# The filter's response of a long convolution as eight quarter products per pair instead of four products with a block matrix

## The chip, the cores and the metric

The kernel runs on one core of a Trainium2 chip. The metric is the device time of one execution in microseconds; smaller is better. TensorE has two rows in the profile: PE, the matmuls, and PEld, the loads of their stationary operands. An fp32 matmul leaves two PE records and two PEld records.

## The reference

Only the first part matters here; a five-tap gate and two 128x128 projections follow it.

```
h_filt = (maximum(pos_emb @ w1, 0) @ w2) * exp(-0.01 * pos)     # [S, D]
u = x * v                                                       # [B, S, D]
y = irfft(rfft(u, 2S) * rfft(h_filt, 2S))[:, :S]                # causal convolution along S
attn = x * y
out = (sigmoid(conv5(attn)) * (attn @ w_val)) @ w_out
B, S, D = 4, 12800, 128;  filter_order = 64
```

## The kernel before

S is split as J x N1 x N2 = 2 x 100 x 64. The kernel has three stages, each with PSUM and SBUF pools of its own, and in each the order of instructions is the order of the code (a manual schedule).

Stage 1 transforms u along N1 and writes the spectra to a_u in HBM. Beside it, it makes ag, the filter's spectrum before the product with w2: for each of the 100 values of k1 a block whose 128 partitions are (j, e), with j the half of S and e one of the 64 hidden units, and whose 128 columns are real and imaginary part (c) of 64 frequencies.

Stage 2 is where the change lies. It loops over 50 pairs of k1. For pair p it does the following, and work of three neighbouring pairs is in flight at once:

- `filter_pair` (L358) makes the filter's response h = w2^T ag for both k1 of the pair. The weights matrix w2bd is 128 x (2 x 128): w2 stands in rows 0 to 63 for j = 0 and in rows 64 to 127 for j = 1, the other half is zeros. Four matmuls of 128 rows, 64 columns of stationary data and 256 streamed columns write one PSUM bank of the pool z_ps. ScalarE (ACT) copies it to h_sb in three instructions (L368, L369 with a sign, L370).
- `spectrum` (L373) finishes the transform of u: two matmuls into one bank of z_ps, four times per pair: z00 (called by `first`), z01 (by `second`), z10 and z11. Each matmul has 128 rows and 64 columns; the two of a spectrum lie beside each other in the array.
- `times` (L379) multiplies spectra and response on VectorE (DVE): va and vb of 2048 elements per partition from z00 and z01, vc and vd of 1024 from z10 and z11. All read one operand from PSUM.
- GpSimd (POOL) adds: L463 the first half of va and vb, L464 vc and vd, L465 the second half of va and vb. DVE then adds the second half of va to vc (L454), from SBUF into SBUF.
- `inverse` (L399) transforms back: from the first half of va (j = 0) and from vc (j = 1), four matmuls of 64 rows and 128 columns each into a two-bank tile of the pool c_ps, and ACT copies the tile to c_sb (L411), which goes to HBM by DMAs on ACT's queue (L414).

The loop's body for p runs on TensorE as z10, z11 of p; the inverse of va of p-1; the response of p+1; z00 of p+1; the inverse of vc of p-1; z01 of p+1. On DVE the row is va, vb of p; L454 of p-1; vc, vd of p. On POOL it is L463, L464, L465 of p. L454 of p-1 needs L465 of p-1.

Stage 3 reads c_y and makes gate and projections. It isn't touched.

Of PSUM z_ps holds four banks (bufs=4, five allocations per pair before the change: h and four spectra) and c_ps two tiles of two banks (bufs=2, two allocations per pair).

Of the kernel before, what the change touches and what calls it, by code (L numbers as in the profile page):

```python
# [9 lines left out]
F32 = mybir.dt.float32  # L10
F32R = mybir.dt.float32r
I32 = mybir.dt.int32
AF = mybir.ActivationFunctionType
# [10 lines left out]
B, S, D, FO, KC = 4, 12800, 128, 64, 5  # L24
J, N1, N2 = 2, 100, 64
# [91 lines left out]
def tile_longconv_gate(  # L117
# [20 lines left out]
    nc = tc.nc  # L138
# [18 lines left out]
    w2bd = const.tile([128, J, D], F32, name="w2bd")  # L157
# [22 lines left out]
    ag = ag_pool.__enter__().tile([128, N1, J, FO], F32, name="ag")  # L180
# [168 lines left out]
    with tc.tile_pool(name="p2", bufs=1) as p2, tc.tile_pool(name="ps2", bufs=1, space=PSUM) as ps2:  # L349
        BD = B * D  # L350
        NP = N1 // 2
        PG = KG // 2
        half = [slice(h * N2, (h + 1) * N2) for h in range(2)]

        def bank():
            return ps2.tile([128, BD], F32, name="z_ps", bufs=4)

        def filter_pair(p):  # L358

            h_ps = bank().rearrange("p (c e) -> p c e", c=2)  # L360
            for c in range(2):
                for h in range(2):
                    nc.tensor.matmul(
                        out=h_ps[half[h], c], lhsT=ag[:, 2 * p + h].rearrange("p j e -> p (j e)")[:, half[c]],
                        rhs=w2bd.rearrange("p j d -> p (j d)"), start=True, stop=True)
            h_sb = p2.tile([128, 2, J, 2, D], F32, name="h_sb2", bufs=3)
            src = h_ps.rearrange("p c (j d) -> p c j d", j=J)
            nc.scalar.copy(out=h_sb[:, 0].rearrange("p j c d -> p c j d"), in_=src)  # L368
            nc.scalar.activation(h_sb[:, 1, :, 0], src[:, 1], AF.Copy, scale=-1.0)  # L369
            nc.scalar.copy(out=h_sb[:, 1, :, 1], in_=src[:, 0])  # L370
            return h_sb

        def spectrum(a2, wk, j, c):  # L373
# [48 lines left out]
        def start_pair(p):  # L422
            filt_p[p] = filter_pair(p).rearrange("p s j c d -> p s (j c) d")
# [9 lines left out]
        with tc.manual_schedule():  # L433
            for p in range(-1, NP + 1):
# [4 lines left out]
                if now:  # L439
                    h = filt_p.pop(p)  # L440
# [35 lines left out]
    with tc.tile_pool(name="p3", bufs=1) as p3, tc.tile_pool(name="ps3", bufs=1, space=PSUM) as ps3:  # L476
# [140 lines left out]
        with tc.manual_schedule():  # L617
# [4 lines left out]
            for _ in range(WARM):  # L622
                w_ps = ps3.tile([D, 2 * D], F32, name="o_ps", bufs=2)
                nc.tensor.matmul(
                    out=w_ps, lhsT=ident, rhs=dft.rearrange("p a k -> p (a k)"), start=True, stop=True)
            for t in range(-AHEAD3, NT + 2):
# [3 lines left out]
                if 0 <= s < NT:  # L630
                    j, g = y_order[s]
# [75 lines left out]
```

## Time and profile before

| what | value |
|---|---|
| median of 3 runs | 1259.43 us (1249.71, 1259.43, 1262.13) |
| the profiled execution | 1253.43 us, of it the span 1251.4 us |
| mean granted TensorE clock | 0.942 |
| stage 2, about | 389 to 832 us of the span |
| busy share of the span | PE 86%, DVE 81%, POOL 70%, ACT 45% |

A profile line of a time table gives start, duration, engine, line, operation, output<-inputs, partitions x elements and count, and in brackets the idle time of the engine before it with what ended it. Matmul ends are modelled by the profile, so starts are compared here.

### The profile page before, as it was taken

The page shows a single profiled execution, that of the slowest core. Times are in us where ns is not written, and L with a number is a line of the kernel's source. Part 1 is how long each engine was busy: PE and PEld are TensorE (multiplying, and loading weights), DVE is VectorE, ACT ScalarE, POOL GpSimd, SP SyncE. Part 2 cuts the span into 40 slices and gives each one's busy share as a digit, 9 for nine tenths or more (in the row PEclk, how much of TensorE's full clock was granted, in tenths as well). Part 3 has the DMA queues.
Part 4 walks back from the last instruction along what each step waited for, and adds up shares of the span by engine and source line. Part 5 has one row for each costly group of instructions (what it writes and reads, how often), then busy time and mean ns, then how long its engine had stood idle before and what let it go on. Part 6 is the DMA issues. An engine that isn't in the chain of part 4 may idle for free. (4 is left out here: it accounts for less than half of the span.)

```text
span 1251.4 us, 15855 instructions
## 1 busy us (share of the span) xinstructions
PE 1073.3 (86%) x5244; PEld 470.7 (38%) x5244; DVE 1014.8 (81%) x1074; ACT 558.7 (45%) x936; POOL 874.0 (70%) x410
## 2 busy tenths in 40 slices
PE   1777787755676999999999999978999999999986
PEld 0544454322333333333333333343444444444432
DVE  7665444747795999999999999933999999999997
ACT  0114433523442333333343333314667667667663
POOL 2435444423452899999999999944888988988980
PEclk9889888858878999999999999988999999999999
DMA  7999999978877687788777777549999999999942
GB/s 181 270 293 360 315 314 304 307 220 275 300 258 280 226 301 274 278 289 285 280 275 272 269 279 273 202 174 258 250 283 278 294 266 269 293 277 281 294 142 106
DMA packets 86794, 333.03 MB, mean 266 GB/s; under 512 B 10062, under 2 KB 11258, under 8 KB 72378
## 3 DMA queue, kind: packets, MB, share of 16 engines
q1 hardware_dynamic: 52736, 252.34, 65.0%
q10 hardware_dynamic: 33978, 79.67, 17.3%
q8 instruction: 44, 0.72, 0.2%
q14 instruction: 36, 0.29, 0.1%
HBM read 200.90 MB, written 131.07 MB: 265 GB/s over the span
## 5 line engine op out<-in xcount | busy, mean ns | idle before, releaser
L565 POOL TENSOR_TENSOR ext<-yr,xr 128x400 f32<-128x400 f32 x120 | 299.4, 2497 | 48.0 <-DVE yr L563 44.8
L286 POOL TENSOR_TENSOR f<-u 128x512 f32<-128x512 f32 x128 | 166.1, 1320 | 219.1 <-DVE u L278 198.5
L296 PE MATMUL fp<-f,fold 64*128 64x512 f32 x512 | 160.3, 738 | 101.9 <-POOL f L286 47.6
L580 DVE SCALAR_TENSOR_TENSOR gt<-ext,cw,gt 128x1600 f32<-128x1600 f32 x128 | 242.6, 1895 | 1.6 <-ACT gt L577 1.6
L411 ACT COPY c_sb<-c_ps 128x1024 f32<-128x1024 f32 x100 | 101.3, 1013 | 270.5 <-PE c_ps L404 266.9
L376 PE MATMUL z_ps<-ld 128*64 128x512 f32 x800 | 194.9, 607 | 6.7 <-DMA ld<-a_u 6.6
L463 POOL TENSOR_TENSOR va<-va,vb 128x1024 f32<-128x1024 f32 x50 | 159.5, 3190 | 38.8 <-DVE vb L381 19.5
L299 ACT COPY st<-fp 128x1024 f32<-128x1024 f32 x64 | 64.8, 1012 | 211.5 <-PE fp L296 110.2
L538 PE MATMUL sd<-ld,inv 100*64 100x512 f32 x512 | 130.1, 612 | 9.4 <-DMA ld<-c_y 8.7
L381 DVE TENSOR_TENSOR vb<-z_ps,h_sb 128x2048 f32<-128x2048 f32 x50 | 114.6, 2291 | 25.2 <-ACT c_sb L411 24.9
L599 PE MATMUL o_ps<-gd,wout 128*128 128x400 f32 x256 | 112.3, 520 | 17.9 <-DVE gd L594 10.4
L464 POOL TENSOR_TENSOR vc<-vc,vd 128x1024 f32<-128x1024 f32 x50 | 118.1, 2361 | 8.7 <-DVE vd L381 3.4
L381 DVE TENSOR_TENSOR va<-z_ps,h_sb 128x2048 f32<-128x2048 f32 x50 | 114.1, 2282 | 11.6 <-PE z_ps L376 11.1
L278 DVE TENSOR_TENSOR u<-ld 128x1024 f32<-128x1024 f32 x64 | 80.6, 1261 | 47.3 <-DMA ld<-in_xv_dram 44.7
L465 POOL TENSOR_TENSOR va<-va,vb 128x1024 f32<-128x1024 f32 x50 | 118.6, 2371 | 0.0
L545 ACT COPY sd_sb<-sd 128x512 f32<-128x512 f32 x128 | 76.2, 595 | 88.1 <-PE sd L538 71.2
L296 PEld LDWEIGHTS fp<-f,fold 64*128 64x128 f32 x512 | 53.2, 217 | 159.2 <-POOL f L286 81.9
L589 PE MATMUL v_ps<-ext,wval 128*128 128x400 f32 x256 | 107.9, 504 | 0.0
L404 PE MATMUL c_ps<-vc,ld 64*128 64x512 f32 x400 | 101.6, 627 | 7.0 <-DVE vc L454 7.0
L301 DVE COPY st<-fp 128x1024 f32<-128x1024 f32 x64 | 78.1, 1220 | 31.7 <-DMA a_u<-st 20.4
L404 PE MATMUL c_ps<-va,ld 64*128 64x512 f32 x400 | 99.4, 615 | 0.1
L376 PEld LDWEIGHTS z_ps<-ld 128*64 128x64 f32 x800 | 54.8, 138 | 111.8 <-issue 86.6
(73 smaller groups left out, 1531.7 us busy)
## 6 DMA issues: line engine op xcount, KB each, us to landing
c_y<-c_sb ACTq DMA_DIRECT2D x100, 512.0 KB
ld<-a_u SPq DMA_DIRECT2D x49, 1024.0 KB
ld<-in_xv_dram SPq DMA_DIRECT2D x64, 768.0 KB
a_u<-st SPq DMA_DIRECT2D x64, 768.0 KB
ld<-c_y SPq DMA_DIRECT2D x128, 384.0 KB
xr<-in_xt_dram SPq DMA_DIRECT2D x32, 800.0 KB
out_dram<-o_sb ACTq DMA_DIRECT2D x32, 800.0 KB
ld<-in_tab_w_dram SPq DMA_DIRECT2D x12, 1024.0 KB
```

The costliest lines, as they stand in the source:

```text
L286: nc.gpsimd.tensor_tensor(f[:, c], u[:, :, 0], u[:, :, 1], op=op)
L296: nc.tensor.matmul(out=fp[:, h], lhsT=fold[r, c], rhs=f[r, c], start=True, stop=True)
L376: nc.tensor.matmul(out=z[half[h]], lhsT=wk[:, h, half[c]], rhs=a2[:, h, j], start=True, stop=True)
L381: nc.vector.tensor_tensor(out, z.rearrange("p (b d) -> p b d", d=D).unsqueeze(1).to_broadcast([128, n, B, D]), h_sb.unsqueeze(2).to_broadc ...
L404: nc.tensor.matmul(out=c_ps[:, h], lhsT=wk[half[h], 2 + c], rhs=vt[half[h], c].rearrange("p b d -> p (b d)"), start=(c == 0), stop=(c == 1))
L463: nc.gpsimd.tensor_tensor(va[:, 0:2], va[:, 0:2], vb[:, 0:2], op=ALU.add)
L464: nc.gpsimd.tensor_tensor(vc, vc, vd, op=ALU.add)
L465: nc.gpsimd.tensor_tensor(va[:, 2:4], va[:, 2:4], vb[:, 2:4], op=ALU.add)
L538: nc.tensor.matmul(out=sd[c * N2:(c + 1) * N2], lhsT=inv[:, c], rhs=ct[c][:, r * B * D:(r + 1) * B * D], start=True, stop=True)
L565: nc.gpsimd.tensor_tensor(e[:, r0 + r], yr, xr, op=ALU.mult)
L580: nc.vector.scalar_tensor_tensor(gt, rows(t, k), cw[:, k:k + 1], gt, op0=ALU.mult, op1=ALU.add)
L599: nc.tensor.matmul(out=o_ps, lhsT=wout, rhs=gd, start=True, stop=True)
```

## The change

The response is made by eight matmuls: each takes 64 rows (one j) and 64 columns (one of c), streams only the 128 columns of w2 that aren't zero, and writes half the partitions of one bank. The two j go to the two banks of a tile from the pool c_ps; the columns 256 to 511 of each bank stay unused. The pool z_ps is left with four allocations per pair, and c_ps has three. ACT's three copies read the new tile in its own order; their element counts stay 512, 256 and 256 per partition. The lines after the new code are one higher: L363 becomes L364, L368 to L370 become L369 to L371, L404 becomes L405, L454 becomes L455 and so on.

```
-            h_ps = bank().rearrange("p (c e) -> p c e", c=2)
+            h_ps = ps2.tile([128, J, BD], F32, name="c_ps", bufs=2)[:, :, 0:2 * D].rearrange("p j (c d) -> p j c d", c=2)
             for c in range(2):
-                for h in range(2):
-                    nc.tensor.matmul(
-                        out=h_ps[half[h], c], lhsT=ag[:, 2 * p + h].rearrange("p j e -> p (j e)")[:, half[c]],
-                        rhs=w2bd.rearrange("p j d -> p (j d)"), start=True, stop=True)
+                for j in range(J):
+                    for h in range(2):
+                        nc.tensor.matmul(
+                            out=h_ps[half[h], j, c],
+                            lhsT=ag[half[j], 2 * p + h].rearrange("p j e -> p (j e)")[:, half[c]],
+                            rhs=w2bd[half[j], j], start=True, stop=True)
             h_sb = p2.tile([128, 2, J, 2, D], F32, name="h_sb2", bufs=3)
-            src = h_ps.rearrange("p c (j d) -> p c j d", j=J)
-            nc.scalar.copy(out=h_sb[:, 0].rearrange("p j c d -> p c j d"), in_=src)
-            nc.scalar.activation(h_sb[:, 1, :, 0], src[:, 1], AF.Copy, scale=-1.0)
-            nc.scalar.copy(out=h_sb[:, 1, :, 1], in_=src[:, 0])
+            nc.scalar.copy(out=h_sb[:, 0], in_=h_ps)
+            nc.scalar.activation(h_sb[:, 1, :, 0], h_ps[:, :, 1], AF.Copy, scale=-1.0)
+            nc.scalar.copy(out=h_sb[:, 1, :, 1], in_=h_ps[:, :, 0])
             return h_sb
```

On TensorE one cycle of stage 2 before, from the inverse of va of one pair on (rows of engine, line, operation, output<-inputs and shape of the output, with the semaphores waited for in brackets):

```order
L404 MATMUL c_ps<-va,ld 128x512 [waits Pool_49]
L404 MATMUL c_ps<-va,ld 128x512 x3
L363 MATMUL z_ps<-w2bd,ag 64x256 [waits DVE_49]
L363 MATMUL z_ps<-w2bd,ag 64x256 x3
L376 MATMUL z_ps<-ld 64x512 [waits DMAHW5_49,DVE_49]
L376 MATMUL z_ps<-ld 64x512
L404 MATMUL c_ps<-vc,ld 128x512 [waits DVE_49,Activation_49]
L404 MATMUL c_ps<-vc,ld 128x512 x3
L376 MATMUL z_ps<-ld 64x512 [waits DVE_49]
L376 MATMUL z_ps<-ld 64x512
L376 MATMUL z_ps<-ld 64x512 [waits DVE_49]
```

and the same place after the change:

```order
L405 MATMUL c_ps<-va,ld 128x512 [waits PE_49,Activation_49,Pool_49]
L405 MATMUL c_ps<-va,ld 128x512 x3
L364 MATMUL c_ps<-w2bd,ag 64x128 [waits Activation_49]
L364 MATMUL c_ps<-w2bd,ag 64x128 x7
L377 MATMUL z_ps<-ld 64x512 [waits DMAHW1_49,DMAHW0_49,DVE_49]
L377 MATMUL z_ps<-ld 64x512
L405 MATMUL c_ps<-vc,ld 128x512 [waits DVE_49,Activation_49]
L405 MATMUL c_ps<-vc,ld 128x512 x3
L377 MATMUL z_ps<-ld 64x512 x2
L377 MATMUL z_ps<-ld 64x512 [waits DVE_49]
L377 MATMUL z_ps<-ld 64x512
```

Nothing changes its place: the response stands between the inverse of va and z00 as before. Its wait is for ACT now (the c_sb copy that frees its tile) instead of DVE, and both inverses wait for the ACT copy that came two allocations earlier.

On ACT the same cycle before, from the copy of the first inverse on:

```order
L411 COPY c_sb<-c_ps 128x2x512 [waits DMAHW6_49,DMAHW5_49,PE_49]
L368 COPY h_sb_2684<-z_ps 128x2x2x128 [waits DVE_49,PE_49]
L369 ACTIVATE h_sb_2684<-z_ps 128x2x128
L370 COPY h_sb_2684<-z_ps 128x2x128
L411 COPY c_sb<-c_ps 128x2x512 [waits PE_49]
```

and after:

```order
L412 COPY c_sb<-c_ps 128x2x512 [waits DMAHW6_49,DMAHW5_49,PE_49]
L369 COPY h_sb_2712<-c_ps 128x512 [waits DVE_49,PE_49]
L370 ACTIVATE h_sb_2712<-c_ps 128x2x128
L371 COPY h_sb_2712<-c_ps 128x2x128
L412 COPY c_sb<-c_ps 128x2x512 [waits PE_49]
```

ACT's row is the same but for the tile that it reads. The rows of DVE and POOL are the same but for line numbers:

```order
L454 TENSOR_TENSOR vc<-vc,va 128x1024 [waits DVE_49,Pool_49]
L381 TENSOR_TENSOR vc<-z_ps,h_sb_2836 128x1024 [waits PE_49]
L381 TENSOR_TENSOR vd<-z_ps,h_sb_2836 128x1024 [waits PE_49]
L381 TENSOR_TENSOR va<-z_ps,h_sb_2886 128x2048 [waits DVE_49,PE_49,Activation_49]
L381 TENSOR_TENSOR vb<-z_ps,h_sb_2886 128x2048 [waits PE_49,Activation_49]
```

This is one cycle of DVE before; L455 and L382 stand in the same row after.

## The prediction

> **What bounds the kernel now.** I read the page first, then the table of stretches for the middle of stage 2, then the order of time of one cycle.
>
> ```profile
> span 1251.4 us, 15855 instructions
> PE 1073.3 (86%) x5244; PEld 470.7 (38%) x5244; DVE 1014.8 (81%) x1074; ACT 558.7 (45%) x936; POOL 874.0 (70%) x410
> ```
>
> ```profile
> 440.00:800.00 360.00, 360.00 (x1712) 124.96 (x1710) 336.77 (x215) 136.01 (x215) 337.95 (x129) 1.00 0.79 277
> ```
>
> The columns of the second are busy time of PE, PEld, DVE, ACT and POOL, the granted clock, the DMA share and GB/s. In the middle of stage 2 PE is never idle, at full clock. But DVE (336.77 of 360, 94%) and POOL (337.95, 94%) stand close behind, so a gain on PE is worth only what these two leave. One cycle in the order of time:
>
> ```profile
> 605.34 2.37 POOL L465 TENSOR_TENSOR va<-va,vb 128x1024 f32<-128x1024 f32 x1
> 605.40 0.14 PEld L376 LDWEIGHTS z_ps<-ld 128*64 128x64 f32 x2 [0.29 <-issue]
> 605.68 2.29 DVE L381 TENSOR_TENSOR vb<-z_ps,h_sb 128x2048 f32<-128x2048 f32 x1 [0.55 <-ACT c_sb L411]
> 605.83 0.14 PEld L376 LDWEIGHTS z_ps<-ld 128*64 128x64 f32 x2 [0.29 <-ACT c_sb L411]
> ...
> 607.22 1.99 PE L404 MATMUL c_ps<-va,ld 64*128 64x512 f32 x8
> ...
> 607.89 1.22 DVE L454 TENSOR_TENSOR vc<-vc,va 128x1024 f32<-128x1024 f32 x1
> 608.12 3.22 POOL L463 TENSOR_TENSOR va<-va,vb 128x1024 f32<-128x1024 f32 x1 [0.41 <-DVE vb L381]
> ...
> 609.02 1.22 DVE L381 TENSOR_TENSOR vc<-z_ps,h_sb 128x1024 f32<-128x1024 f32 x1
> ...
> 609.13 1.08 PE L363 MATMUL z_ps<-w2bd,ag 128*64 128x256 f32 x8
> 609.25 1.01 ACT L411 COPY c_sb<-c_ps 128x1024 f32<-128x1024 f32 x1 [3.63 <-PE c_ps L404]
> ...
> 610.05 1.03 PE L376 MATMUL z_ps<-ld 128*64 128x512 f32 x4
> 610.16 1.22 DVE L381 TENSOR_TENSOR vd<-z_ps,h_sb 128x1024 f32<-128x1024 f32 x1
> ...
> 611.00 1.99 PE L404 MATMUL c_ps<-vc,ld 64*128 64x512 f32 x8
> 611.02 0.38 ACT L370 COPY h_sb<-z_ps 128x256 f32<-128x256 f32 x1
> 611.29 2.28 DVE L381 TENSOR_TENSOR va<-z_ps,h_sb 128x2048 f32<-128x2048 f32 x1
> 611.45 2.36 POOL L464 TENSOR_TENSOR vc<-vc,vd 128x1024 f32<-128x1024 f32 x1
> ...
> 612.92 2.79 PE L376 MATMUL z_ps<-ld 128*64 128x512 f32 x12
> 613.04 1.01 ACT L411 COPY c_sb<-c_ps 128x1024 f32<-128x1024 f32 x1 [1.64 <-PE c_ps L404]
> ...
> 613.77 2.37 POOL L465 TENSOR_TENSOR va<-va,vb 128x1024 f32<-128x1024 f32 x1
> ...
> 614.12 2.29 DVE L381 TENSOR_TENSOR vb<-z_ps,h_sb 128x2048 f32<-128x2048 f32 x1 [0.55 <-ACT c_sb L411]
> ...
> 615.65 1.56 PE L404 MATMUL c_ps<-va,ld 64*128 64x512 f32 x6
> ...
> 616.33 1.22 DVE L454 TENSOR_TENSOR vc<-vc,va 128x1024 f32<-128x1024 f32 x1
> ```
>
> From 607.22 to 615.65 is one cycle of 8.43 us, and five bursts of PE abut in it. DVE stands still once, 0.55 before vb. The copy named there isn't vb's source: vb reads z01, whose two steps are the first third of the burst at 612.92, so this is DVE waiting for PE.
>
> A second loop is hidden behind it. L454 needs POOL's L465 of the pair before; vc, vd, L464 and L465 follow L454; and the next L454 follows L465. By starts: L454 at 607.89, L465 at 613.77 plus 2.37 is 616.14, which is 8.25 after it. L454 then starts at 616.33, with vb (614.12 + 2.29 = 616.41, overlapped by the usual 0.08), so POOL has 0.19 to spare there, less the time from L465's end to L454's start.
>
> **The change, on PE.** Two PEld rows of two loads each lie 0.43 apart (605.40, 605.83): the two matmuls beside each other go through in steps of 0.43 for 512 columns, and so 0.215 for 256 and 0.107 for 128 (an estimate in proportion). Against these steps each burst has an overhead: the z burst at 612.92 has six steps, 2.58, and takes 2.73 to 615.65; the z burst at 610.05 has two, 0.86, and takes 0.95; the response has four of 0.215, 0.86, and takes 0.92; an inverse has four, 1.72, and takes 1.92. So leaving an arrangement of the array (128 rows by 64 columns, or 64 by 128) costs about 0.10, entering the first 0.05 and the second 0.10. Between the response and z00 nothing is due now: both have 128 rows by 64 columns.
>
> After the change the response has 64 by 64. Eight matmuls of two records, four beside each other, are four steps of 0.107, 0.43 in place of 0.86: −0.43. It enters and leaves as before, but z00 behind it must be entered again: +0.10 for leaving, +0.05 for entering. PE's cycle becomes 8.43 − 0.43 + 0.15 = 8.15. No row shows four matmuls beside each other, so the bounds are wide: the switch lies between 0 and the inverse's 0.20, and if only two run together the steps take 0.86 as before; PE's cycle lies between 8.00 and 8.63. I take 8.15, since pairs beside each other in columns (z) and in rows (the inverses) both show a full overlap, and the quarters are both at once.
>
> The Trainium skill ("TensorE: Matmul & The Clock Gate", section "Part 3: Packing small matmuls — row/col tiling") says that matmuls start and end strictly in program order. By that rule the second record of one quarter would hold up the next quarter, which is the third rival below. The trace speaks against it: under it the burst of six steps would have seven and take 3.0, and it takes 2.73.
>
> **The change, on the waits.** The inverse of vc must now wait for the copy that frees the tile of the inverse of va: that ends at 609.25 + 1.01 = 610.26, and PE would come there at 611.00 − 0.28 = 610.72, 0.46 later. Behind it z01, z10 and z11 queue, and vb waits for them; with this cover the wait costs nothing. The inverse of va waits for the copies of the response (611.02 + 0.38 = 611.40), which is four microseconds early, and the response for the copy that began at 613.04, which is over 3 us early. Each spectrum now takes the bank of the same spectrum one pair earlier; the tightest, z10, is freed by vc at 610.24 and is needed near 613.5. ACT's copies keep their sizes and cost nothing: ACT was busy 136 of 360. DMA issues stay as they are.
>
> **What is late next.** At 8.15 the loop through POOL no longer fits: it takes 8.25 plus the time from L465 to L454. For that time, and for what happens then, the trace has one place, at the start of stage 2:
>
> ```profile
> 409.15 2.28 DVE L381 TENSOR_TENSOR vb<-z_ps,h_sb 128x2048 f32<-128x2048 f32 x1
> 409.57 2.38 POOL L465 TENSOR_TENSOR va<-va,vb 128x1024 f32<-128x1024 f32 x1
> ...
> 411.89 2.37 POOL L463 TENSOR_TENSOR va<-va,vb 128x1024 f32<-128x1024 f32 x1
> 411.98 3.35 DVE L454 TENSOR_TENSOR vc<-vc,va 128x1024 f32<-128x1024 f32 x1 [0.56 <-POOL va L465]
> ...
> 415.26 1.21 DVE L381 TENSOR_TENSOR vc<-z_ps,h_sb 128x1024 f32<-128x1024 f32 x1
> ...
> 415.39 3.14 PE L404 MATMUL c_ps<-vc,ld 64*128 64x512 f32 x8 [2.83 <-DVE vc L454]
> ...
> 419.99 2.37 POOL L465 TENSOR_TENSOR va<-va,vb 128x1024 f32<-128x1024 f32 x1
> 420.14 2.29 DVE L381 TENSOR_TENSOR vb<-z_ps,h_sb 128x2048 f32<-128x2048 f32 x1 [0.34 <-issue]
> ...
> 422.39 1.23 DVE L454 TENSOR_TENSOR vc<-vc,va 128x1024 f32<-128x1024 f32 x1
> 422.51 3.34 POOL L463 TENSOR_TENSOR va<-va,vb 128x1024 f32<-128x1024 f32 x1 [0.15 <-DVE vb L381]
> ```
>
> L465 ends at 411.95 and L454 starts 0.03 later, so the loop is 8.25 + 0.03 = 8.28. And here L463 began 0.09 ahead of L454: L463 took its plain 2.37, and L454 took 3.35 instead of 1.22, ending 1.07 after L463. In the steady cycle L454 is ahead, by 0.23 (607.89, 608.12); there L454 keeps its 1.22 and L463 takes 3.22. The two don't run together, and the one that starts first holds the other up. With L454 ahead the 0.85 falls into POOL's slack; with L463 ahead 2.13 falls on DVE, and the cycle is the one from 411.98 to 422.39, 10.41.
>
> L463 starts 0.15 behind vb or right behind L465 (411.89 lies 0.06 before L465's end), whichever is later; L454 starts with vb's end or 0.03 behind L465. While PE sets the pace at 8.43, vb is late, POOL is done, and L454 wins by 0.23. At 8.15 L465 falls back by 8.28 − 8.15 = 0.13 each cycle; after the lead of 0.23, within two cycles, L463 wins. Then the late L454 makes the next L464 and L465 late too, so L463 wins again: the order feeds itself.
>
> What ends it is PE's clock. In a turned cycle PE waits about 10.41 − 8.15 = 2.26 in one piece for L454. The stretches around two such idle spans:
>
> ```profile
> 166.92:170.33 3.41, 1.50 (x10) 0.78 (x8) 1.34 (x2) 1.77 (x2) 2.49 (x2) 1.00 0.96 336
> 170.33:173.74 3.41, 3.41 (x34) 2.50 (x32) 1.87 (x2) 0.66 (x1) 1.41 (x2) 0.50 0.83 298
> 412.68:416.09 3.41, 0.70 (x4) 0.47 (x6) 3.41 (x2) 0.19 (x1) 1.58 (x1) 1.00 0.29 115
> 416.09:419.50 3.41, 3.41 (x11) 0.80 (x10) 3.41 (x3) 0.93 (x1) 1.82 (x1) 0.50 0.00 0
> ```
>
> A stretch of 3.41 with PE busy 1.50 or less is followed by one at half clock. At 416.09 that made the inverse of vc 3.07 long (415.39 to 418.46) and vb late (420.14, 0.34 idle), so that L454 came first again at 422.39. 2.26 of idle time leaves 1.15 of a stretch, under 1.50, if it lies wholly in it: with up to 0.35 cut off, in (3.41 − 2.26 + 0.70) / 3.41, about half of the placings (an estimate). So I take two turned cycles, then a half-clock stretch, then two good ones of 8.28: the mean is (2 × 8.28 + 2 × 10.41) / 4 = 9.35, 0.92 above 8.43. Over the 49 cycles between 50 pairs that is +45. The sum is made against the profiled execution, 1253.43, which lies 0.5% under the median 1259.43 (the spread of the runs may itself be the number of turned cycles at the start, 2.0 each): 1253.4 + 45 = **1298**. One turned cycle for two good ones gives 8.99, +27, 1281; three for one give 9.88, +71, 1324.
>
> **Rivals.**
>
> - *L454 keeps its lead.* Slower PE steps (a gain of 0.15 or less), or a tie that falls to DVE, leave the cycle at 8.28: −0.15 × 49 = −7, **1246**. For it: the lead is decided by 0.1 us, and one place shows who wins. Against it: the lag grows each cycle. It decides at a PE cycle of 8.28; above, nothing turns.
> - *The quarters run two at a time*, so the change doesn't do what it says: eight steps of 0.107 and the switch, PE cycle 8.58, +0.15 × 49 = +7, **1261**. For it: no row shows four. Against it: the pairs overlap fully in both directions.
> - *The quarters go in program order*, the second record of each ahead of the first of the next: nine steps, 0.96 in place of 0.86, and the switch, PE cycle 8.68, +0.25 × 49 = +12, **1266**. Against it: the z burst of 2.73, which would be 3.0. This is the rule of the Trainium skill's page on TensorE named above.
> - *The turned order never ends*: 10.41 − 8.43 = 1.98 in 49 cycles, +97, **1350**. For it: idle spans of 2.26 are shorter than the 2.83 at 415.39. Against it: 1.50 busy was enough at 166.92. The Trainium skill ("TensorE: Matmul & The Clock Gate", section "Part 1: The HAM clock gate") gives half clock after a whole idle window of about 3.4 us; by that rule 2.26 idle would never do, and this rival would hold. The stretch at 166.92 disagrees with it.
>
> **How the numbers follow.** Forecast 0.64, L454 keeps its lead 0.16, two at a time 0.13, program order 0.03, never ends 0.04. The forecast's own range is 1281 to 1324. The range for all, 1246 to 1330, reaches from the first rival through the second and third, and leaves out half of the first and all of the last. A measurement of this kernel can tell about 1% from no change. Slower by over 1% is the forecast and the last rival, 0.68. The first rival is 0.6% under the profiled execution and 1.1% under the median, so it is split: faster 0.09; within 1% its other part, two at a time and program order, 0.23.
>
> **What would show it.** The eight quarter matmuls should fill some 0.5 us of a cycle, with PE idle before the inverse of vc. L455 should show a mean far above 1.22, near 2.2, with a longest near 3.4, and L464 (L463 before) a mean below 3.22. Starts of L455 should lie 10.4 apart in some cycles and 8.3 in others, and the granted clock in stage 2 should drop from 1.00. If L455 stays at 1.22 throughout, the turning is wrong; if the response takes 0.9 or more, the four beside each other are.

## The result and the profile after

The median of four runs of the changed kernel is **1295.87 us** (1294.93 to 1297.40), against 1256.82 (1249.71 to 1262.13) before in the same comparison: a ratio of **1.032 [1.026, 1.037]**, slower. The forecast was 1298, with "slower by over 1%" at 0.68. The profiled execution took 1297.40; before it took 1253.43.

The head of the page after:

```profile
span 1295.3 us, 16655 instructions
...
PE 1072.3 (83%) x5644; PEld 463.6 (36%) x5644; DVE 1066.2 (82%) x1074; ACT 553.7 (43%) x936; POOL 855.0 (66%) x410
```

DVE is busy 51 us longer (1014.8 before) though it has the same 1074 instructions. Something on DVE takes longer; nothing was added. The table of stretches for the middle of stage 2 (columns as in the prediction):

```profile
440.00:800.00 360.00, 329.22 (x1840) 110.71 (x1832) 345.68 (x193) 117.51 (x192) 284.94 (x115) 0.95 0.72 253
```

PE, which filled all 360.00 before, now idles 31 of 360, at a mean clock of 0.95 in place of 1.00. DVE is busier than before, POOL (284.94, 337.95 before) and ACT (117.51, 136.01) do less work in the same time. The table of groups says where the DVE time sits (shapes, count, busy time and mean of one, idle time before and what ended it):

```profile
L455 DVE TENSOR_TENSOR vc<-vc,va 128x1024 f32<-128x1024 f32 x50 | 115.0, 2300 | 12.7 <-POOL va L466 12.2
...
L464 POOL TENSOR_TENSOR va<-va,vb 128x1024 f32<-128x1024 f32 x50 | 140.1, 2802 | 25.8 <-DMA ld<-a_u 19.4 <-DVE vb L382 4.6
...
L405 PE MATMUL c_ps<-vc,ld 64*128 64x512 f32 x400 | 113.5, 688 | 45.1 <-DVE vc L455 45.1
```

Before, the same two adds were

```profile
L463 POOL TENSOR_TENSOR va<-va,vb 128x1024 f32<-128x1024 f32 x50 | 159.5, 3190 | 38.8 <-DVE vb L381 19.5
...
L454 DVE TENSOR_TENSOR vc<-vc,va 128x1024 f32<-128x1024 f32 x50 | 62.9, 1258 | 5.3 <-POOL va L465 5.3
```

So the mean of the DVE add went from 1258 ns to 2300, POOL's add beside it got cheaper (2802, 3190 before), and PE waits 45.1 us for the DVE add. The view of the one line shows that 2300 is a mean of two kinds (shortest, median, longest; first and last start), where before all but one had the short form:

```profile
L454 DVE TENSOR_TENSOR vc<-vc,va x50: 1214/1215/3354, 412.0 to 827.0; 128x1024 f32<-128x1024 f32 x50
...
L455 DVE TENSOR_TENSOR vc<-vc,va x50: 1214/2286/3424, 410.8 to 872.3; 128x1024 f32<-128x1024 f32 x50
```

The last start is 872.3; before it was 827.0. The whole loss lies ahead of it: what follows the last start takes 423.0 here and 424.4 before. Call a cycle, from one start of this add to the next, turned where the add has the long form, and good where it has the short one. Of the 49 cycles between the 50 starts, 25 are turned, with a mean of 10.50 us, and 24 are good, with 8.29. One round of the pattern, in order of time, is two turned cycles and two good ones:

```profile
586.34 2.37 POOL L466 TENSOR_TENSOR va<-va,vb 128x1024 f32<-128x1024 f32 x1
...
588.72 2.35 POOL L464 TENSOR_TENSOR va<-va,vb 128x1024 f32<-128x1024 f32 x1
588.75 3.40 DVE L455 TENSOR_TENSOR vc<-vc,va 128x1024 f32<-128x1024 f32 x1 [0.17 <-POOL va L466]
...
592.29 1.99 PE L405 MATMUL c_ps<-vc,ld 64*128 64x512 f32 x8 [0.89 <-DVE vc L455]
...
599.14 2.35 POOL L464 TENSOR_TENSOR va<-va,vb 128x1024 f32<-128x1024 f32 x1
599.22 3.36 DVE L455 TENSOR_TENSOR vc<-vc,va 128x1024 f32<-128x1024 f32 x1 [0.41 <-POOL va L466]
...
602.73 2.92 PE L405 MATMUL c_ps<-vc,ld 64*128 64x512 f32 x8 [2.19 <-DVE vc L455]
...
605.57 3.51 PE L377 MATMUL z_ps<-ld 128*64 128x512 f32 x12
...
607.49 2.29 DVE L382 TENSOR_TENSOR vb<-z_ps,h_sb 128x2048 f32<-128x2048 f32 x1 [0.45 <-PE z_ps L377]
...
609.01 1.99 PE L405 MATMUL c_ps<-va,ld 64*128 64x512 f32 x8
...
609.70 1.22 DVE L455 TENSOR_TENSOR vc<-vc,va 128x1024 f32<-128x1024 f32 x1
609.92 3.22 POOL L464 TENSOR_TENSOR va<-va,vb 128x1024 f32<-128x1024 f32 x1 [0.33 <-DVE vb L382]
...
610.93 0.67 PE L364 MATMUL c_ps<-w2bd,ag 64*64 64x128 f32 x16
...
611.53 1.08 PE L377 MATMUL z_ps<-ld 128*64 128x512 f32 x4
...
617.18 1.99 PE L405 MATMUL c_ps<-va,ld 64*128 64x512 f32 x8
...
617.99 1.23 DVE L455 TENSOR_TENSOR vc<-vc,va 128x1024 f32<-128x1024 f32 x1
618.09 3.36 POOL L464 TENSOR_TENSOR va<-va,vb 128x1024 f32<-128x1024 f32 x1
```

Read the pairs of L464 and L455. At 588.72 and 599.14 POOL starts first, by 0.03 and 0.08 us; POOL's add then takes 2.35 and DVE's 3.40 and 3.36, and PE's inverse of vc waits 0.89 and 2.19. At 609.70 and 617.99 DVE starts first, by 0.22 and 0.10; DVE's add takes 1.22 and POOL's 3.22 and 3.36. A tenth of a microsecond decides about two.

Between the turned and the good cycles lies the inverse at 602.73, which takes 2.92 in place of 1.99. The table of stretches, cut where the granted clock changes:

```profile
590.00:593.41 3.41, 2.52 (x26) 1.09 (x20) 3.41 (x3) 1.90 (x4) 1.07 (x1) 1.00 0.87 316
...
600.24:603.65 3.41, 1.22 (x6) 0.55 (x6) 3.41 (x3) 0.79 (x3) 1.26 (x1) 1.00 1.04 415
603.65:607.06 3.41, 3.41 (x10) 0.93 (x8) 3.39 (x3) 1.01 (x1) 2.14 (x1) 0.50 0.25 101
```

The stretch with the wait of 0.89 has PE busy 2.52 and the clock stays at 1.00 after it. The one with the wait of 2.19 has PE busy 1.22, and the next 3.41 us run at 0.50. That also accounts for the round: four cycles of PE's own 8.17 are 32.68, the two waits add 3.08, and a stretch at half clock loses half of itself, 1.71; the sum is 37.47, and the round measures 37.54 (from the start of L455 at 572.16 to that four cycles later, at 609.70).

### The profile page after: what moved, and what is told of

Same layout as the page of the kernel before. It is cut to its first block, busy times and chain, and to the rows that moved or that the text cites. A ratio compares the mean times of both kernels' runs of the same rounds, so it can differ in the third digit from the quotient of the medians.

```text
span 1295.3 us, 16655 instructions
## 1 busy us (share of the span) xinstructions
PE 1072.3 (83%) x5644; PEld 463.6 (36%) x5644; DVE 1066.2 (82%) x1074; ACT 553.7 (43%) x936; POOL 855.0 (66%) x410
## 5 line engine op out<-in xcount | busy, mean ns | idle before, releaser
L296 PE MATMUL fp<-f,fold 64*128 64x512 f32 x512 | 155.8, 719 | 105.1 <-ACT st L299 50.0
L377 PE MATMUL z_ps<-ld 128*64 128x512 f32 x800 | 204.7, 631 | 7.7 <-DMA ld<-a_u 7.1
L464 POOL TENSOR_TENSOR va<-va,vb 128x1024 f32<-128x1024 f32 x50 | 140.1, 2802 | 25.8 <-DMA ld<-a_u 19.4
L405 PE MATMUL c_ps<-vc,ld 64*128 64x512 f32 x400 | 113.5, 688 | 45.1 <-DVE vc L455 45.1
L455 DVE TENSOR_TENSOR vc<-vc,va 128x1024 f32<-128x1024 f32 x50 | 115.0, 2300 | 12.7 <-POOL va L466 12.2
L382 DVE TENSOR_TENSOR vb<-z_ps,h_sb 128x2048 f32<-128x2048 f32 x50 | 114.3, 2286 | 11.3 <-PE z_ps L377 4.9
L382 DVE TENSOR_TENSOR va<-z_ps,h_sb 128x2048 f32<-128x2048 f32 x50 | 113.8, 2276 | 11.2 <-PE z_ps L377 11.2
L466 POOL TENSOR_TENSOR va<-va,vb 128x1024 f32<-128x1024 f32 x50 | 118.2, 2364 | 0.0
L405 PE MATMUL c_ps<-va,ld 64*128 64x512 f32 x400 | 100.2, 620 | 0.0
```

Of the source, the lines that this page charges most:

```text
L296: nc.tensor.matmul(out=fp[:, h], lhsT=fold[r, c], rhs=f[r, c], start=True, stop=True)
L377: nc.tensor.matmul(out=z[half[h]], lhsT=wk[:, h, half[c]], rhs=a2[:, h, j], start=True, stop=True)
L382: nc.vector.tensor_tensor(out, z.rearrange("p (b d) -> p b d", d=D).unsqueeze(1).to_broadcast([128, n, B, D]), h_sb.unsqueeze(2).to_broadc ...
L405: nc.tensor.matmul(out=c_ps[:, h], lhsT=wk[half[h], 2 + c], rhs=vt[half[h], c].rearrange("p b d -> p (b d)"), start=(c == 0), stop=(c == 1))
L464: nc.gpsimd.tensor_tensor(va[:, 0:2], va[:, 0:2], vb[:, 0:2], op=ALU.add)
```

## The experiments

The theory is that of the prediction: PE's cycle fell below the loop that runs from the DVE add L455 over vc, vd and two POOL adds to the next L455; the lead of L455 over L464 was lost, and the two adds hold each other up in the dear order. The rivals are that the new tile (another pool, other waits) costs the time, that the quarters themselves are dear on PE, and that the loop's length alone does it, without the holding up. The kernel before took 1251.70 in the session of the first four experiments and 1251.56 in that of the last three; the ratios are to it. The changed kernel didn't run again in these two sessions, so differences to it go by the 1295.87 above.

### The tile alone: e1_tile_only

The block products stay; only the response's place in PSUM changes, from the spectra's pool to the inverse's.

```
-            h_ps = bank().rearrange("p (c e) -> p c e", c=2)
+            h_ps = ps2.tile([128, 2, BD], F32, name="c_ps", bufs=2)[:, :, 0:2 * D]
```

> The four block products of before, but written into a tile of the inverse's pool c_ps (the pool move alone). Theory (PE's faster cycle turns the order of the VectorE add L455 and the GpSimd add L464): PE's cycle stays 8.43, nothing turns, and the time is that of before, 1250 to 1262. Rival 1 (the third allocation in a pool of two tiles makes the inverses wait for ACT): as slow as after, about 1296. Rival 2 (eight small products and their switches cost PE time): as before.

Measured: 1252.12 (1248.86 to 1259.79), ratio 0.9996 [0.996, 1.003]. In the middle of stage 2 PE is full, as before:

```profile
440.00:800.00 360.00, 360.00 (x1710) 124.79 (x1710) 336.70 (x215) 136.00 (x215) 338.30 (x129) 1.00 0.78 277
```

The cycle is 8.43 and one of 49 is turned, as before. So at this pace the pools and their waits cost nothing; e4_swap below shows the same at the pace of the changed kernel.

### The change with more work on PE: e2_more_pe

The quarters of c = 0 are made twice, so that PE has twelve quarter products instead of eight.

```
-            for c in range(2):
+            for c in (0, 0, 1):
```

> The changed kernel with the four quarter products of c = 0 made twice: 200 more matmuls, two more steps of 0.107 per cycle. Theory: PE's cycle goes from 8.17 to 8.385, above the loop of 8.28, so the order doesn't turn after the first cycle: 1253.4 - 0.05 x 49 = 1251 (1249 to 1256), 45 us faster than after by doing more. Rival 1: unchanged waits, 1296 or more. Rival 2: 1296 + 0.215 x 49 = 1307.

Measured: 1249.85 (1244.80 to 1252.32), ratio 0.996 [0.993, 1.000]. With 50% more of the very work that the change was about, the kernel is 46 us faster than the changed one. The one line:

```profile
L455 DVE TENSOR_TENSOR vc<-vc,va x50: 1212/1215/3346, 411.5 to 824.3; 128x1024 f32<-128x1024 f32 x50
```

One add of 50 is long. The cycle is 8.385, which is 0.21 above the 8.17 of eight quarters, as four more of them in two steps of 0.107 give; and it lies above the loop's 8.28, and nothing turns. The quarters aren't dear; PE's being too quick is what costs.

### Before with less work on PE: e3_less_pe

The other direction, in the old kernel: the first inverse leaves out the second half of its sum, four of its eight matmuls, 0.86 us of a cycle by the steps of 0.43. Its sum is thus another one.

```
-            for c in range(2):
+            terms = (0,) if j == 0 else (0, 1)
+            for c in terms:
...
-                        start=(c == 0), stop=(c == 1))
+                        start=(c == 0), stop=(c == terms[-1]))
```

> The kernel before, block products and all, with half of the first inverse's matmuls left out (the accumulation over c for j = 0), which takes two steps of 0.43 off PE's cycle: 8.43 - 0.86 = 7.57. Theory: L463 wins, about three cycles of four turned, 1253.4 + 49 x ((8.28 + 3 x 10.43) / 4 - 8.43) = 1324 (1295 to 1340), slower with 43 us less of PE work. Rivals 1 and 2: neither the pool nor the products changed, so 1253 or, down to the loop of 8.28, 1246.

Measured: 1320.58 (1309.62 to 1324.00), ratio **1.053 [1.045, 1.062]**: 43 us of work less on PE (50 × 0.86), and the kernel takes 69 us longer.

```profile
440.00:800.00 360.00, 301.08 (x1322) 99.34 (x1320) 343.41 (x184) 116.00 (x184) 269.09 (x111) 0.93 0.69 244
...
L455 DVE TENSOR_TENSOR vc<-vc,va x50: 1214/3350/3382, 403.0 to 882.1; 128x1024 f32<-128x1024 f32 x50
```

The median of the add is the long form; 33 of 49 cycles are turned (10.49 in the mean; the profiled execution, 1309.62, is the shortest of the five). Neither quarter products nor the new tile are in this kernel, and it shows the same loss, larger. So the loss goes with PE's pace and not with how the response is made.

### The change with the loop cut: e4_swap

The last two POOL adds change places: the second half of va, for which L455 waits, no longer stands behind the add of vc and vd, which waits for DVE's vc and vd.

```
                     nc.gpsimd.tensor_tensor(va[:, 0:2], va[:, 0:2], vb[:, 0:2], op=ALU.add)
-                    nc.gpsimd.tensor_tensor(vc, vc, vd, op=ALU.add)
                     nc.gpsimd.tensor_tensor(va[:, 2:4], va[:, 2:4], vb[:, 2:4], op=ALU.add)
+                    nc.gpsimd.tensor_tensor(vc, vc, vd, op=ALU.add)
```

> The changed kernel with POOL's last two adds exchanged (second half of va and vb before vc and vd). Theory: the add of va no longer stands behind vd, the loop L455, vc, vd, L465, L466 is cut, POOL alone needs about 8.0, L455 keeps its lead of 0.23 and the cycle is PE's 8.17: 1253.4 - 0.26 x 49 = 1241 (1236 to 1244), and no turned cycle. Rivals 1 and 2: nothing on PE or in the pool changes, 1296.

Measured: **1237.15** (1236.62 to 1238.78), ratio to before **0.986 [0.980, 0.992]**, and 58.7 us under the changed kernel. It is the fastest of all that ran. In the middle of stage 2:

```profile
440.00:800.00 360.00, 360.00 (x2118) 122.26 (x2116) 347.59 (x221) 134.91 (x220) 347.02 (x133) 1.00 0.79 279
...
L464 POOL TENSOR_TENSOR va<-va,vb 128x1024 f32<-128x1024 f32 x44 | 141.6, 3219 | 13.0 <-DVE vb L382 13.0
...
L455 DVE TENSOR_TENSOR vc<-vc,va 128x1024 f32<-128x1024 f32 x44 | 53.5, 1215 | 0.0
```

PE is full again at full clock, at a cycle of 8.17, L455 never waits, and L464 pays the 3.22 from its slack each time. The expectation of no turned cycle at all was off by one: the one at the start of stage 2 is still there (longest L455 3345). The gain that PE's shorter cycle promises, 49 × (8.43 − 8.17) = 12.7, is here in full: 1251.70 − 1237.15 = 14.6, within the spread of the kernel before (and 11.3 under the kernel before with the same exchange, the next experiment). The new tile with its three allocations stands in this kernel too, so its waits cost nothing at 8.17 either.

### Before with the same exchange: e5_swap_block

The same edit in the old kernel.

> The kernel before with POOL's last two adds exchanged, the block products kept. Theory: PE sets the pace at 8.43 in both, so only the turned cycles of the start go away (2.0 each, one to six by the spread of before): 1248 to 1252. If instead the exchange by itself were the gain, it would come near the 1237 of the exchange with quarter products.

Measured: 1248.42 (1244.36 to 1274.81), ratio 0.996 [0.993, 1.000]; the cycle stays 8.43, and one of 49 is turned. The exchange by itself gives at most 0.8%. So nearly all of its 58.7 us above comes from cutting the loop, and with it the turned order, and is not a gain of its own.

### The change with the loop, without the holding up: e6_no_lock

L455 takes its first operand from PSUM (the spectrum z10) instead of from vc in SBUF. It still waits for POOL, still has the loop, but reads one operand from SBUF instead of two. It computes another sum.

```
-                    nc.vector.tensor_tensor(oc, oc, oa[:, 2:4], op=ALU.add)
+                    nc.vector.tensor_tensor(
+                        oc, z10.rearrange("p (b d) -> p b d", d=D).unsqueeze(1).to_broadcast([128, 2, B, D]),
+                        oa[:, 2:4], op=ALU.add)
```

> The changed kernel where the VectorE add L455 takes the spectrum z10 from PSUM in place of vc from SBUF: it has one operand in SBUF, the same duration class, and still waits for L466. (The sum is another one than the reference's; everything else is kept.) Theory: L455 and L464 no longer hold each other up, so L464 takes 2.37 in every cycle and L455 1.22, nothing turns, and what is left is the loop over L455, vc, vd, L465, L466: cycles of 8.28, 1253.4 - 0.15 x 49 - 2 = 1244 (1240 to 1248), PE idle 0.11 per cycle. If the late start of L455 behind L466 were the cost and not the holding up, it would stay near 1296.

Measured: 1242.70 (1239.81 to 1246.84), ratio 0.992 [0.990, 0.995]; 1244 was expected. Two cycles in order of time (POOL's three adds are L466, L467, L468 here):

```profile
601.27 2.38 POOL L466 TENSOR_TENSOR va<-va,vb 128x1024 f32<-128x1024 f32 x1
601.35 1.23 DVE L455 TENSOR_TENSOR vc<-z_ps,va 128x1024 f32<-128x1024 f32 x1 [0.42 <-POOL va L468]
...
609.57 2.38 POOL L466 TENSOR_TENSOR va<-va,vb 128x1024 f32<-128x1024 f32 x1
609.65 1.23 DVE L455 TENSOR_TENSOR vc<-z_ps,va 128x1024 f32<-128x1024 f32 x1 [0.42 <-POOL va L468]
```

POOL starts 0.08 ahead, in the order that costs 2 us in the changed kernel, and both adds take their plain time beside each other; it is so in all 49 cycles (POOL ahead by 0.06 to 0.10, no add of DVE over 1.23). The starts are 8.30 apart: this is the loop alone, and it would have been 1243 us, slightly faster than before. The other 53 us of the changed kernel are the holding up; its 25 turned cycles give about the same, 25 × (10.50 − 8.29) = 55. The rows of the kernel before in the prediction agree: the multiplications, which read one operand from PSUM, run beside POOL's adds at their plain times (va of 2.28 at 611.29 beside L464 of 2.36 at 611.45). The Trainium skill ("SBUF — State Buffer", section "Who interferes with whom") says that a VectorE instruction with two inputs in SBUF contends with GpSimd's reads, that one with a single SBUF input doesn't, and that the order of issue decides who blocks; the trace agrees, with 1.23 beside 2.38 here, and with 3.40 beside 2.35 or 1.22 beside 3.22 where both inputs are in SBUF.

### A dose between: e7_half_dose

The changed kernel, with extra quarter products of c = 0 over 64 of the 128 columns: half of the extra work of e2_more_pe, so that PE's cycle comes to lie right at the loop's.

```
-            for c in range(2):
+            for c, n in ((0, D // 2), (0, D), (1, D)):
...
-                            out=h_ps[half[h], j, c],
+                            out=h_ps[half[h], j, c, 0:n],
...
-                            rhs=w2bd[half[j], j], start=True, stop=True)
+                            rhs=w2bd[half[j], j, 0:n], start=True, stop=True)
```

> The changed kernel with the quarter products of c = 0 made once more over 64 of their 128 columns: PE's cycle 8.17 + 0.107 = 8.28, at the loop's 8.28. Theory: L466 falls back by some 0.01 a cycle, so long runs of good cycles and some turned ones, between the whole dose (1250) and none (1296): 10 to 17 turned cycles, 1268 to 1285. A cost of the products themselves would give 1296 + 5 = 1301.

Measured: 1260.43 (1251.17 to 1273.87), ratio 1.005 [1.000, 1.009]. It lies between the doses, 1295.87 with none and 1249.85 with the whole, but below the 1268 to 1285 that was expected. The profiled execution is the longest of ten, 1273.87, so its count stands for no other, and it serves here only to show how the order comes and goes:

```profile
L455 DVE TENSOR_TENSOR vc<-vc,va x50: 1215/1226/3426, 412.3 to 847.7; 128x1024 f32<-128x1024 f32 x50
```

In it 13 of 49 cycles are turned: one at the start, two from 556.43 on and ten from 718.46 on. Between them the good cycles take 8.30, and the lead of L455 falls from 0.23 to nothing, first in 13 of them and then in 16, that is 0.01 to 0.02 in each (some 0.01 was expected). The sign of the dose is as the theory has it, its size was missed. How many cycles turn in an execution near the median was not seen, so why there are fewer than expected is open.

## Why the prediction was right

**PE's cycle.** Forecast 8.15; two inverses of va with no wait between them start at 609.01 and 617.18, so 8.17. The response starts at 610.93 and z00 at 611.53: 0.60, forecast 0.58 (four steps of 0.107 and the new switch of 0.15), against 0.92 before. So four quarters do run beside each other, and "two at a time" and "program order" fall with it.

**The waits cost nothing.** e1_tile_only shows it at a cycle of 8.43, and e4_swap, where PE fills 360.00 of 360, at 8.17.

**The loop.** Forecast 8.28, measured 8.29 in the good cycles of the kernel after and 8.30 in e6_no_lock, where nothing else is in play. That it decides is shown from both sides: more PE work mends the changed kernel (e2_more_pe), less PE work harms the old one (e3_less_pe), and cutting the loop gives 1237 (e4_swap).

**The holding up.** Forecast from one place at the start of stage 2: 3.35 against 1.22, turned cycles of 10.41. Measured: 3.35 to 3.42 and 10.50; e6_no_lock shows that the holding up goes when one of the add's two operands comes from PSUM, and that without it the loss isn't there. "L454 keeps its lead" fell: with a lead lost by tenths, POOL won in 25 of 49 cycles.

**What ends it.** "Two turned cycles, then two good ones" came out, with a mean of 37.54 / 4 = 9.39 against 9.35, but the working had a wrong step. It put the idle time of PE at 2.26 in every turned cycle and got the two from a chance of one half that it falls into one stretch. In the trace PE, still late from the half-clock stretch before, waits only 0.89 in the first turned cycle and 2.19 in the second; the first leaves its stretch busy 2.52 and the clock alone, the second leaves 1.22. So the number two follows from the two waits, not from a chance, and that the forecast had it too was luck. (PE's waits for L455 between 440 and 840 fit this in every round:

```profile
PE c_ps L405 <- DVE vc L455: 33.9, 22, 2.2
```

22 waits, 11 of each kind: 11 × (0.89 + 2.19) = 33.9.) "The turned order never ends" fell. That the half clock is the cause of the return rests on traces alone. In the changed kernel each return in stage 2 comes with a half-clock stretch, and in it z01 is late and vb waits 0.45 for it (607.49), which lets POOL finish first. In e3_less_pe 16 half-clock stretches begin between 403 and 862 us, and the order returns 16 times, each time at the first add after one. And where no such stretch falls, the order stays turned: in e3_less_pe from 421.71 to past 473.88, for six adds in a row, and in the execution of e7_half_dose from 718.46 to past 791.55, for eight (the first line is of e3_less_pe, the second of e7_half_dose, both at a clock of 1.00 throughout):

```profile
417.20:478.60 61.40, 45.53 (x216) 15.27 (x216) 58.89 (x30) 18.97 (x30) 41.82 (x18) 1.00 0.63 225
728.00:796.40 68.40, 53.85 (x374) 19.38 (x372) 65.50 (x34) 20.45 (x34) 45.25 (x20) 1.00 0.62 212
```

One half-clock stretch is not always enough: in e7_half_dose the one at 796.47 leaves the order turned, and the next, at 816.95, ends it. Nor is the prediction's limit of 1.50 a sharp one: in e3_less_pe the clock stayed at 1.00 after stretches with PE busy 1.45 (464.98) and 1.49 (601.51), and before the change it fell to 0.50 after one with 1.69 (129.37). No experiment held the clock, so the cause of the return stays open.

**The sum.** 49 × (9.39 − 8.43) = 47 against 45 in the forecast. Between the first and the last start of the add the traces differ by 46.5 (461.5 after, 415.0 before); the parts of the span ahead of these starts and behind them were 2.6 shorter after the change, which the forecast did not have. The cycles cost 1.5 more than the 45 and the rest 2.6 less, so that the profiled execution came out at 1297.40 for 1298; that it is so near is in part luck.

## What to carry to other kernels

Before an engine that sets the pace is made faster, follow the loop that comes next through the other engines, and look for pairs of instructions there that hold each other up: which of them starts first may hang on a lead of tenths of a microsecond that the slow engine provided. Here a mean duration that nearly doubled with the count unchanged (1258 to 2300 ns) was such a pair turned round, and the view of the one line (shortest, median, longest) showed it as two kinds. The remedy here was not to take the gain back but to cut the loop: two lines exchanged on POOL turned +3.2% into −1.4%.

## What was not expected of the hardware

A round of four cycles comes out at almost the length of 11 of the clock's stretches of 3.413. The half-clock stretches in the middle of stage 2 begin at 453.46, 491.01, 528.55, 566.10, 603.65 and 641.19, each 37.54 or 37.55 after the last, and so on to 866.47, with four cycles between them every time.

```profile
603.65:607.06 3.41, 3.41 (x10) 0.93 (x8) 3.39 (x3) 1.01 (x1) 2.14 (x1) 0.50 0.25 101
607.06:641.19 34.13, 31.05 (x186) 10.69 (x184) 32.65 (x19) 11.25 (x19) 27.86 (x12) 1.00 0.76 269
641.19:644.61 3.42, 3.42 (x10) 0.92 (x8) 3.38 (x3) 1.01 (x1) 2.15 (x1) 0.50 0.22 87
```

Between two half-clock stretches lie 34.13 us at full clock, with PE idle 3.08 of them, the two waits of a round. One might take the pattern to be locked to the clock, but it drifts past it:

```profile
449.08 3.35 DVE L455 TENSOR_TENSOR vc<-vc,va 128x1024 f32<-128x1024 f32 x1 [0.40 <-POOL va L466]
...
861.95 3.35 DVE L455 TENSOR_TENSOR vc<-vc,va 128x1024 f32<-128x1024 f32 x1 [0.41 <-POOL va L466]
```

These are the second turned adds of the first round and of the twelfth. The first starts 4.38 us ahead of its half-clock stretch (453.46), the other 4.52 ahead (866.47), and in the rounds between the distance grows by about 0.01 each time: a round takes 37.53, and 11 stretches take 37.55. The two are so nearly alike that twelve rounds pass without a cycle more or less. The runs of the changed kernel agree within 0.2% (1294.93 to 1297.40) though each is full of close races, which fits with so regular a pattern; that it causes this was not tried.
